# The last group's three output stores: from SyncE's queue to GpSimd's and ScalarE's, the last copy shared by two engines

## The chip, the cores and the metric

The kernel runs on one core of a Trainium2 chip. The metric is the device time of one execution in microseconds, over runs of the same program. Besides the runs there is one execution taken by the hardware profiler, with its own time and its own span.

A core has five engines that run side by side, each with its own instruction stream: TensorE (PE in the profile: matmuls, and PEld for their weight loads), VectorE (DVE), ScalarE (ACT), GpSimd (POOL) and SyncE (SP). They wait for each other through semaphores. A transfer between memory and the core's buffers (a DMA) is issued by an instruction on SyncE, ScalarE or GpSimd. The profile names an engine with a q behind it (SPq, POOLq, PEldq) where it means its instruction queue: issues of transfers, waits, branches and the like.

## The reference

An RWKV attention with a decaying state, and behind it a two-layer feed-forward network on its output:

```python
for t in range(S):                                   # batch 4, 8 heads, 768 steps, head size 48
    cur = np.einsum('bhd,bhe->bhde', u[None] * kt, vt)
    y[:, :, t] = np.einsum('bhd,bhde->bhe', rt, state + cur)
    state = wt[:, :, :, None] * state + np.einsum('bhd,bhe->bhde', kt, vt)

h = x @ w_in                                         # x: 3072 tokens x 384, w_in: 384 x 2048
g = h * (1.0 / (1.0 + np.exp(-1.702 * h)))
return (g @ w_out).astype(np.float32)                # w_out: 2048 x 384
```

Everything is float32. The output is 3072 x 384 floats; the kernel writes it transposed, as three blocks of 128 features by 3072 tokens (`out_t`).

## The kernel before

The 3072 tokens are 24 chunks of 128, and four chunks make a group of 512 tokens: six groups. The attention of a chunk leaves its output in the tile `x` of its group. The feed-forward of a group is cut into 16 tasks, one for each 128 of the 2048 hidden features: the first product (`first_product` or `first_rows`, into PSUM tile `ph`), the gelu on ScalarE and VectorE (`gelu`, L383 to L385), and the second product (`second_product`, L398 to L400, or `second_rows`, L424), which adds into three PSUM tiles of the group, `po0`, `po1` and `po2`, each 128 features by 512 tokens. The list `TASKS` has 106 tasks. The order of all pieces is written out: by the string `RAMP` at the start, then by the generator `rest()`, whose tokens (`l` load, `a` attention, `g`, `h`, `y`, `r` for the products and the gelu) are run one by one by `do`.

When the last task of a group has gone through the second product, `do` calls `store` (L493). It takes the three `po` tiles in turn: ScalarE copies and rescales one into an SBUF tile `ob` (L498, one of three buffers), and a transfer of 256 KB takes `ob` to the output (L499). For five groups the products run in halves of the array (`r` tokens) and the order of the tiles is 1, 0, 2; for the last group it is `y105` that ends it, with the order 0, 1, 2. Of this last group the matmuls of `po0`, `po1` and `po2` end one after the other, so the three copies follow them at the very end of the program.

Which queue issues a transfer is set by `queue[0]`. In the loop over `rest()` it is GpSimd's, except for tokens of the last task:

```python
queue[0] = G if int(token[1:]) < len(TASKS) - 1 else nc.sync     # L605
```

So the stores of groups 1 to 4 go through GpSimd (12 of them; those of group 0 fall in `RAMP`, which uses SyncE), and those of group 5 through SyncE.

Behind the loop stands a test that was computed long before (L613 to L622): each engine loads a count from memory (L622, TENSOR_LOAD) and compares (L623, COMPARE_BRANCH). For these inputs every engine jumps over the whole slow path, some hundred lines of code, to the end of the program. There each engine settles the semaphores that it owns: SyncE those of the transfers by SyncE and ScalarE (L623 EVENT_SEMAPHORE, eight of them), GpSimd those of its own transfers (four waits and an INC_SWDGE_SEM at L623). Then SyncE waits for all of them (L720) and a rendezvous of all five engines, led by GpSimd, ends the program: each engine runs a DRAIN and reports, GpSimd collects the reports and lets all go. SyncE's resets can't pass a transfer by SyncE or ScalarE that has not landed, and SyncE's waits at L720 can't pass GpSimd's INC_SWDGE_SEM.

The program is scheduled by hand: the instructions of an engine stand in the order in which the tokens emit them, and the framework adds the waits.

Of the kernel before, what the change touches and what calls it, by code (L numbers as in the profile page):

```python
# [13 lines left out]
AF = mybir.ActivationFunctionType  # L14
ALU = mybir.AluOpType
# [5 lines left out]
NTOK = B * S  # L21
# [20 lines left out]
W_SCALE = 2.0 ** 8  # L42
# [8 lines left out]
TASKS = [(0, 0, 2, f) for f in range(5)]  # L51
# [35 lines left out]
def rwkv_ffn_kernel(ctx: ExitStack, tc, wkr, vp, vrk, ub, w_in, w_out, masks, vt, uc, out):  # L87
    nc = tc.nc
    V, A, G, T = nc.vector, nc.scalar, nc.gpsimd, nc.tensor
# [24 lines left out]
        out=after, in_=after, pattern=[[1, C]], base=0, channel_multiplier=-1,  # L114
# [6 lines left out]
    queue = [nc.sync]  # L121
# [371 lines left out]
    def store(i, start, N, order=range(NM)):  # L493

        for m in order:
            o = po[i][m]
            ob = pools["late"].tile([P, WIDE], F32, tag="ob", name="ob", bufs=3)[:, 0:N]
            A.activation(ob, o[:, 0:N], AF.Copy, scale=1.0 / W_SCALE)  # L498
            queue[0].dma_start(out[m, :, bass.ds(start, N)], ob)  # L499
        po.pop(i)  # L500
        xs.pop(i)

# [4 lines left out]
    with tc.manual_schedule():  # L507
# [17 lines left out]
        def do(token):  # L525
            kind, i = token[0], int(token[1:] or 0)
            told[token] = told.get(token, 0) + 1
            if kind in "lamwr":
                piece(kind, i)
                if kind == "w" and all(told.get(f"w{n}") == 4 for n in range(2 * NL)):  # L530
                    early.close()
                    pools["late"] = fast.enter_context(tc.tile_pool(name="late", bufs=2))
            elif kind == "f":
                fetch(i)
            elif kind == "x":
                group, col = where[i]
                if i == 1:
                    fill_x(xs[group], 0, 2 * C)
                elif i == 3:
                    fill_x(xs[group], 2 * C, 4 * C)  # L540
                elif col == CHUNKS[group] - 1:
                    fill_x(xs[group], 0, (col + 1) * C)
            elif kind == "u":
                nc.sync.dma_start(u_sb, ub)
            elif kind == "M":
                A.dma_start(hm[0:D], masks[0:D])
                A.dma_start(hm[HB:R2], masks[D:R])
                for sf in states:
                    G.memset(sf, 0.0)
            elif kind == "k":  # L550
                for _ in range(i):
                    keep_clock()
            elif kind == "g":
                first_product(i, TASKS[i])
            elif kind == "h":
                gelu(i, TASKS[i])
            elif kind == "y":
                second_product(i, TASKS[i])
            if kind == "y" or kind == "r" and told[token] == 2:
                i -= LAG if kind == "r" else 0  # L560
                parts.pop(i, None)
                group = TASKS[i][0]
                if i == last[group]:
                    store(group, starts[group] * C, CHUNKS[group] * C, (1, 0, 2) if kind == "r" else range(NM))

        def rest():

            begins = []
            for t, (i, col) in enumerate(where):
                n = len([x for x in TASKS if x[0] == i - 1])  # L570
                begins.append(last.get(i - 1, -1) + 1 - BEFORE - round((CHUNKS[i] - 1 - col) * n / CHUNKS[i]))
            done, plan = dict(told), {}
            for t, begin in enumerate(begins):
                late = 0
                for kind, step, half in PARTS:
                    token = f"{kind}{t + 2 * (kind == 'l')}"
                    if done.get(token, 0):
                        done[token] -= 1
                    elif kind != "l" or t + 2 < NT:
                        at_ = 2 * (step + begin) + half  # L580
                        if at_ < 2 * FIRST:
                            at_ = 2 * FIRST + late
                            late += 1
                        plan.setdefault(at_, []).append(token)
            for j in range(FIRST, len(TASKS) + LAG):
                for post in range(2):
                    if post and j <= SPLIT[-1] + 1:
                        yield f"r{j}"
                        if j > SPLIT[0]:
                            yield f"h{j - 1}"  # L590
                    if post and j < len(TASKS) and j not in SPLIT:
                        yield f"g{j}"
                        yield f"h{j}"
                    yield from plan.get(2 * j + post, ())
                if j <= SPLIT[-1] + 1:
                    yield f"r{j}"
                elif f"y{j - LAG}" not in told:
                    yield f"y{j - LAG}"
# [3 lines left out]
        steady.append(True)  # L602
        tiled.append(True)
        for token in rest():
            queue[0] = G if int(token[1:]) < len(TASKS) - 1 else nc.sync  # L605
            do(token)
        queue[0] = nc.sync

# [13 lines left out]
    n = nc.values_load(cnt, min_val=0, max_val=full)  # L622
    with tc.If(n < full):  # L623
# [5 lines left out]
        with tc.tile_pool(name="gp", bufs=1) as gp, tc.tile_pool(name="ob", bufs=2) as ob, tc.For_i(0, B, 1) as b:  # L629
# [33 lines left out]
            for half in range(2):  # L663
                xs[half] = xg[half]
                for f in range(NF):
                    task = half, 0, 3, f
                    first_product(f, task)
                    gelu(f, task)
                    second_product(f, task)
                store(half, b * S + half * 384, 384)  # L670
# [54 lines left out]
```

## Time and profile before

| what | us |
|---|---|
| median of 3 runs | 537.95 (537.9 to 539.91) |
| the profiled execution's own time | 539.33 |
| its span, first to last instruction | 537.7 |
| PE busy | 522.9 (97%) |
| ACT / DVE / POOL busy | 285.5 / 294.5 / 58.7 |
| last matmul ends, about | 530.6 |
| last copy of `po` on ScalarE | 530.64 to 531.25 |
| last store issued on SyncE's queue | 531.9 |

A row of a group view has the line, the engine, the operation, and the tile written with what is read, then the count. In the view of one source line the columns are the least, median and longest duration in nanoseconds, then the start of the first and of the last of these instructions in microseconds from the span's start. In the timeline and the chain of waits the first two numbers are start and duration in microseconds. A semaphore instruction's start is the moment its waits were fulfilled, so time spent waiting shows as a gap in front of it and not as its duration.

### The profile page before, as it was taken

To read this page: it belongs to the slowest core of one execution; us is meant where nothing else is said; L and a number is where in the kernel's file an instruction comes from. 1 tells how busy PE (TensorE), PEld (TensorE's weight loads), DVE (VectorE), ACT (ScalarE), POOL (GpSimd) and SP (SyncE) were. 2 spreads that over 40 slices of the span, in tenths; PEclk is the share of its full clock that TensorE was granted. 3 is DMA by queue.
4 is the path that set the end of the run, shared out by engine and by line. 5 is a ranking of instruction groups with operands and counts; after the bars stand their busy time and mean duration, and the time that the engine had idled before them with its cause. 6 is when DMAs were issued, how large, how long until landed. Compare 5 with 4: busy or idle time off the path is not lost.

```text
span 537.7 us, 11653 instructions
## 1 busy us (share of the span) xinstructions
PE 522.9 (97%) x4750; PEld 442.9 (82%) x4750; DVE 294.5 (55%) x454; ACT 285.5 (53%) x629; POOL 58.7 (11%) x119
## 2 busy tenths in 40 slices
PE   6999899999999999999999999999999999999994
PEld 2667799988888888788999999988999887888873
DVE  3999788989765471664564554566466321211210
ACT  1889678987564364465355365454464432322222
POOL 5030110000100001030003030103020002100000
PEclk9999989999999999999999999999999999999998
DMA  8979949333632431163211354213250001100001
GB/s 202 236 189 204 320 110 183 74 89 103 180 88 67 96 95 29 47 173 79 53 45 37 91 155 98 53 46 69 58 155 1 1 1 30 59 3 2 1 1 64
DMA packets 15308, 48.26 MB, mean 90 GB/s; under 512 B 3024, under 2 KB 5264, under 8 KB 15248
## 3 DMA queue, kind: packets, MB, share of 16 engines
q0 software_dynamic: 6368, 23.73, 18.7%
q1 hardware_dynamic: 8624, 23.42, 16.8%
q8 instruction: 39, 0.64, 0.5%
q10 hardware_dynamic: 256, 0.30, 0.3%
q14 instruction: 21, 0.17, 0.1%
HBM read 40.36 MB, written 4.72 MB: 84 GB/s over the span
## 4 chain that ended last, share of the span: by engine, by line
PE 92%; DVE 4%; DMA 1%; ACT 1%; POOL 1%; issue 1%; DVEq 0%; SPq 0%; POOLq 0%
PE po L424 26%; PE ph L424 24%; PE ph L372 4%; PE ps_y L335 4%; PE po L398 4%; PE ps_s L322 4%; PE ph L373 4%; PE ph L374 4%; PE po L400 4%; PE po L399 4%; PE idle L413 4%; PE ps_y L342 3%; PE ps_u L307 1%; DMA x<-x 1%; PE ps_d L260 1%; PE ps_t L286 1%
## 5 line engine op out<-in xcount | busy, mean ns | idle before, releaser
L424 PE MATMUL ph<-x,pair 64*128 64x512 f32 x1134 | 194.0, 387 | 0.0
L385 DVE TENSOR_TENSOR gl<-gf,gh 128x512 fp32r<-128x512 f32 (+1 forms) x106 | 67.5, 639 | 193.7 <-ACT gf L384 193.7
L424 PE MATMUL po<-gh,pair 64*128 64x512 f32 x768 | 164.6, 396 | 0.2 <-SPq L429 0.2
L424 PEld LDWEIGHTS ph<-x,pair 64*128 64x128 f32 x1134 | 146.5, 184 | 14.7
L383 ACT ACTIVATE gh<-ph 128x512 fp32r<-128x512 f32 (+1 forms) x106 | 59.0, 556 | 179.1 <-PE ph L424 149.9
L424 PEld LDWEIGHTS po<-gh,pair 64*128 64x128 f32 x768 | 96.5, 185 | 11.8 <-issue 1.2
L424 PE MATMUL po<-gl,pair 64*128 64x512 f32 x384 | 103.0, 388 | 0.0
L297 ACT ACTIVATE am<-ident,s 128x128 f32<-128x128 f32 x192 | 58.9, 393 | 2.5 <-PE ps_y L335 2.5
L384 ACT ACTIVATE gf<-ph 128x512 f32<-128x512 f32 (+1 forms) x106 | 58.5, 552 | 0.0
L424 PEld LDWEIGHTS po<-gl,pair 64*128 64x128 f32 x384 | 50.2, 184 | 6.0
L372 PE MATMUL ph<-x,pair 128*128 128x512 f32 (+1 forms) x129 | 46.3, 359 | 2.4 <-DMA x<-x 2.4
L373 PE MATMUL ph<-x,pair 128*128 128x512 f32 (+1 forms) x129 | 44.6, 345 | 0.0
L374 PE MATMUL ph<-x,pair 128*128 128x512 f32 (+1 forms) x129 | 44.5, 345 | 0.0
L398 PE MATMUL po<-gh,pair 128*128 128x512 f32 (+1 forms) x126 | 44.0, 349 | 0.1
L400 PE MATMUL po<-gl,pair 128*128 128x512 f32 (+1 forms) x126 | 42.8, 340 | 0.0
L399 PE MATMUL po<-gh,pair 128*128 128x512 f32 (+1 forms) x126 | 42.7, 339 | 0.0
L325 DVE COPY_PREDICATED am<-after,ps_s 128x512 f32<-128x512 int32 x48 | 32.6, 732 | 3.8 <-PE ps_s L322 3.3
L360 POOL DMA_DIRECT2D x<-x x30 | 15.3, 516 | 163.4 <-DVE x L203 163.4
L232 DVE TENSOR_TENSOR_SCAN lp<-wkr_t,d1r 112x516 f32<-112x516 f32 x24 | 29.5, 1229 | 5.1 <-POOL d1r L106 4.4
L413 PE MATMUL idle<-d1r 112*128 112x512 bf16 x107 | 27.4, 403 | 4.4 <-POOL d1r L106 4.4
L372 PEld LDWEIGHTS ph<-x,pair 128*128 128x128 f32 x129 | 25.0, 194 | 6.7 <-issue 3.6
L238 DVE TENSOR_TENSOR_SCAN lp<-wkr_t,d1f 112x516 f32<-112x516 f32 x24 | 29.5, 1230 | 0.5
(75 smaller groups left out, 666.2 us busy)
## 6 DMA issues: line engine op xcount, KB each, us to landing
wkr_t<-in_wkr POOLq DMA_DIRECT2D x23, 288.9 KB, 6.2
raw<-in_w_out SPq DMA_DIRECT2D x6, 1024.0 KB, 17.4
wkr_t<-in_wkr SPq DMA_DIRECT2D x14, 385.2 KB, 5.2
wkr_t<-in_wkr POOLq DMA_DIRECT2D x9, 385.2 KB, 5.1
rk_t<-in_vrk POOLq DMA_DIRECT2D x9, 384.0 KB, 5.5
out_t<-ob POOLq DMA_DIRECT2D x12, 256.0 KB, 2.8
v_t<-in_vrk SPq DMA_DIRECT2D x15, 192.0 KB, 6.2
rk_t<-in_vrk SPq DMA_DIRECT2D x7, 384.0 KB, 4.2
```

Of the source, the lines that this page charges most:

```text
L297: A.activation(x_[:, p], ident, AF.Copy, scale=s[:, 2 * p + h : 2 * p + h + 1])
L372: T.matmul(ph, h_, xs[i][:, 0, c, cs], start=c == 0, stop=False)
L373: T.matmul(ph, h_, xs[i][:, 1, c, cs], start=False, stop=False)
L374: T.matmul(ph, l_, xs[i][:, 0, c, cs], start=False, stop=c == NM - 1)
L383: A.activation(gh, ph, AF.Gelu_apprx_sigmoid, scale=1.0 / W_SCALE)
L384: A.activation(gf, ph, AF.Gelu_apprx_sigmoid, scale=1.0 / W_SCALE)
L385: V.tensor_tensor(gl, gf, gh.bitcast(F32), op=ALU.subtract)
L398: T.matmul(o, h_, gh, start=first, stop=False, skip_group_check=True)
L399: T.matmul(o, l_, gh, start=False, stop=False, skip_group_check=True)
L400: T.matmul(o, h_, gl, start=False, stop=f == NF - 1, skip_group_check=True)
L413: T.matmul(out, zeros[:, 0:P], zeros[:, 0:WIDE], start=first, stop=first, skip_group_check=True)
L424: mm = T.matmul(out, w[rows], x[rows], start=start, stop=stop, skip_group_check=True)
```

## The change

All in the last group's stores. `queue[0]` stays GpSimd's for the last task too, so the copies of `po0` and `po1` are stored through GpSimd's queue. The last tile, `po2`, is copied in two halves of 256 columns: ScalarE does the left half, VectorE the right half, both into the same `ob` tile. Its store is issued from ScalarE's queue. SyncE issues no store of the last group. The slow path is not touched, since `start` isn't an integer there.

```diff
@@ store
         for m in order:
             o = po[i][m]
             ob = pools["late"].tile([P, WIDE], F32, tag="ob", name="ob", bufs=3)[:, 0:N]
-            A.activation(ob, o[:, 0:N], AF.Copy, scale=1.0 / W_SCALE)
-            queue[0].dma_start(out[m, :, bass.ds(start, N)], ob)
+            end = m == order[-1] and isinstance(start, int) and start + N == NTOK
+            n = N // 2 if end else N
+            A.activation(ob[:, 0:n], o[:, 0:n], AF.Copy, scale=1.0 / W_SCALE)
+            if end:
+                V.tensor_scalar(ob[:, n:], o[:, n:N], 1.0 / W_SCALE, None, op0=ALU.mult)
+            (A if end else queue[0]).dma_start(out[m, :, bass.ds(start, N)], ob)
         po.pop(i)
         xs.pop(i)
@@ the loop over rest()
         for token in rest():
-            queue[0] = G if int(token[1:]) < len(TASKS) - 1 else nc.sync
+            queue[0] = G
             do(token)
```

Lines behind the edit move by four: L622 of before is L626 of the change, L623 is L627, L720 is L724, and L498 and L499 are L500 and L503.

How the instructions stand on three engines at the program's end follows. DMASW and DMAHW in the waits are counts of landed transfers (GpSimd's, and those of SyncE and ScalarE).

GpSimd, from the stores of the fifth group (`ob` filled from `po` of group 4) to its branch. Before:

```order
L499 DMA out_t<-ob 128x512 [waits DMASW5_49,Activation_49]
L499 DMA out_t<-ob 128x512 [waits DMASW6_49,Activation_49]
L499 DMA out_t<-ob 128x512 [waits DMASW7_49,Activation_49]
L622 TENSOR_LOAD acc [waits DVE_49,Activation_49,Pool_49]
L623 COMPARE_AND_BRANCH
```

With the change:

```order
L503 DMA out_t<-ob 128x512 [waits DMASW5_49,Activation_49]
L503 DMA out_t<-ob 128x512 [waits DMASW6_49,Activation_49]
L503 DMA out_t<-ob 128x512 [waits DMASW7_49,Activation_49]
L503 DMA out_t<-ob 128x512 [waits DMASW0_49,Activation_49]
L503 DMA out_t<-ob 128x512 [waits DMASW1_49,Activation_49]
L626 TENSOR_LOAD acc [waits DVE_49,Activation_49,Pool_49]
L627 COMPARE_AND_BRANCH
```

Two stores of the last group now stand ahead of GpSimd's load, its branch and all that it does behind the branch.

ScalarE, from the last gelu to its branch, before and with the change:

```order
L384 ACTIVATE gf<-ph 128x512 [waits DVE_49]
L498 ACTIVATE ob<-po_5959 128x512 [waits DMASW5_49,PE_49]
L498 ACTIVATE ob<-po_5945 128x512 [waits DMASW6_49,PE_49]
L498 ACTIVATE ob<-po_5961 128x512 [waits DMASW7_49,PE_49]
L622 TENSOR_LOAD acc [waits DVE_49,Activation_49,Pool_49]
L623 COMPARE_AND_BRANCH
```

```order
L384 ACTIVATE gf<-ph 128x512 [waits DVE_49]
L500 ACTIVATE ob<-po_5959 128x512 [waits DMASW5_49,PE_49]
L500 ACTIVATE ob<-po_5945 128x512 [waits DMASW6_49,PE_49]
L500 ACTIVATE ob<-po_5961 128x256 [waits DMASW7_49,PE_49]
L503 DMA out_t<-ob 128x512 [waits DMAHW4_49,DVE_49]
L626 TENSOR_LOAD acc [waits DVE_49,Activation_49,Pool_49]
L627 COMPARE_AND_BRANCH
```

The third copy is half as wide, and a store that waits for VectorE stands between it and ScalarE's load and branch.

VectorE at the same place has one new row, and SyncE has lost three. VectorE with the change, then SyncE before and with it:

```order
L385 TENSOR_TENSOR gl<-gf,gh 128x512 [waits PE_49,Activation_49] x18
L502 TENSOR_SCALAR ob<-po_5961 128x256 [waits DMASW7_49,DMAHW2_49,DMASW2_49,Activation_49]
L626 TENSOR_LOAD acc [waits DVE_49,Activation_49,Pool_49]
L627 COMPARE_AND_BRANCH
```

```order
L622 ISA x2
L499 DMA out_t<-ob 128x512 [waits PE_49,DMAHW4_49,Activation_49]
L499 DMA out_t<-ob 128x512 [waits DMAHW5_49,Activation_49]
L499 DMA out_t<-ob 128x512 [waits DMAHW6_49,Activation_49]
L623 COMPARE_AND_BRANCH
```

```order
L626 ISA x2
L627 COMPARE_AND_BRANCH [waits PE_49]
```

VectorE's half waits for ScalarE and not for TensorE: the count of ScalarE's that it waits for is the one that the left half sets. SyncE's branch has no store ahead of it any more.

## The prediction

> **What bounds the kernel now.** I read the page first, then the chain of waits at the end, then the queues' views of the lines at the end.
>
> ```profile
> span 537.7 us, 11653 instructions
> PE 522.9 (97%) x4750; PEld 442.9 (82%) x4750; DVE 294.5 (55%) x454; ACT 285.5 (53%) x629; POOL 58.7 (11%) x119
> PE 92%; DVE 4%; DMA 1%; ACT 1%; POOL 1%; issue 1%; DVEq 0%; SPq 0%; POOLq 0%
> ```
>
> TensorE is busy for 97% of the span and carries 92% of the chain. The change touches none of its work, so nothing before the last copies can move. What is at stake is the tail. The chain's last pieces (start, duration, what), and SyncE's timeline over the whole tail and from 531 us on:
>
> ```profile
> 530.38 0.24 PE po L400
> 530.62 0.02 issue
> 530.64 0.60 ACT ob L498
> ...
> 529.91 2.33 SPq L499 DMA_DIRECT2D out_t<-ob  x3
> ...
> 530.59 1.66 SPq L499 DMA_DIRECT2D out_t<-ob  x2
> ```
>
> The last matmul ends at 530.62 and the last copy at 530.64 + 0.60 = 531.24. The span ends at 537.7, so 6.5 us of tail follow. The view of L499 in the last 10 us (least, median, longest ns, first and last start), and below it the same line around 468 us, where the fifth group was stored by GpSimd:
>
> ```profile
> L499 SPq DMA_DIRECT2D out_t<-ob x3: 342/383/1179, 529.9 to 531.9; - x3
> DMA to landing us min/median/max: 3.0/3.0/3.4
> ...
> L499 POOL DMA_DIRECT2D out_t<-ob x3: 542/564/573, 467.0 to 468.3; - x3
> DMA to landing us min/median/max: 2.3/2.6/3.0
> ```
>
> The second store's issue began at 530.59, the third's at 531.9 and lasted 383 ns: one issue took 1179 ns and held the third back by 0.65 us after its data was ready. The third landed by 531.9 + 3.0 = 534.9. Was that what SyncE waited for? The view of the branch line, queue by queue:
>
> ```profile
> L623 SPq EVENT_SEMAPHORE  x8: 17/17/17, 535.5 to 536.0; - x8
> L623 POOLq EVENT_SEMAPHORE  x4: 17/43/43, 469.5 to 471.3; - x4
> L623 POOLq COMPARE_BRANCH  x1: 58/58/58, 469.0 to 469.0; - x1
> L623 POOLq INC_SWDGE_SEM  x1: 2276/2276/2276, 471.4 to 471.4; - x1
> L623 DVEq COMPARE_BRANCH  x1: 72/72/72, 528.4 to 528.4; - x1
> L623 PEldq COMPARE_BRANCH  x1: 3822/3822/3822, 529.1 to 529.1; - x1
> L623 DVEq EVENT_SEMAPHORE  x1: 21/21/21, 531.5 to 531.5; - x1
> L623 ACTq COMPARE_BRANCH  x1: 45/45/45, 531.5 to 531.5; - x1
> L623 ACTq EVENT_SEMAPHORE  x1: 17/17/17, 532.0 to 532.0; - x1
> L623 SPq COMPARE_BRANCH  x1: 53/53/53, 532.3 to 532.3; - x1
> L623 PEldq EVENT_SEMAPHORE  x1: 51/51/51, 533.0 to 533.0; - x1
> ```
>
> No. SyncE branches at 532.3, behind its third store, and its next instruction runs at 535.5: a jump of 3.2 us, 0.6 longer than the landing. VectorE's and TensorE's jumps also take 3.1 (528.4 to 531.5) and 3.9 us (529.1 to 533.0); ScalarE's and GpSimd's take 0.5. So SyncE's late branch bounds the tail: 532.3, jump to 535.5, eight resets to 536.1, then twelve waits, and the rendezvous:
>
> ```profile
> L720 SPq EVENT_SEMAPHORE  x14: 17/28/28, 536.1 to 537.6; - x14
> L720 POOLq EVENT_SEMAPHORE  x4: 17/17/17, 536.9 to 537.6; - x4
> L720 POOLq DRAIN  x3: 50/107/8556, 473.7 to 537.4; - x3
> L720 SPq DRAIN  x3: 7/7/13, 536.8 to 537.1; - x3
> ```
>
> GpSimd collects the reports at 536.9, and the program ends 0.8 us later. The row to look at is the third: of GpSimd's three DRAINs one took 8.556 us. It is the one at 473.7, just behind INC_SWDGE_SEM (471.4 + 2.28 = 473.7), and it ended at 482.3, with 54 us to spare. GpSimd had issued its last transfer at 468.3.
>
> **The change part by part.** The sum is made against the profiled execution: span 537.7, own time 539.33, which is 1.4 above the median of 537.95. A shift of the span is added to the median.
>
> *SyncE loses three issues.* Its last work before them is the relay of TensorE's split tasks, at 524.3:
>
> ```profile
> L429 SPq EVENT_SEMAPHORE  x7: 17/17/28, 519.2 to 524.3; - x7
> ```
>
> It branches there, and its 3.2 us jump is over at 527.6, before the first of the last copies. This takes the present end of the chain off the path. What is late next, in turn:
>
> *Copy and store of po2.* These rows price them:
>
> ```profile
> L384 ACT ACTIVATE gf<-ph 128x256 f32<-128x256 f32 x20 | 7.6, 380 | 0.0
> L385 DVE TENSOR_TENSOR gl<-gf,gh 128x256 fp32r<-128x256 f32 x20 | 8.2, 416 | 5.8 <-ACT gf L384 5.8
> L613 DVE TENSOR_SCALAR acc<-acc 128x48 f32<-128x48 f32 x1 | 0.2, 180 | 0.0
> L127 ACTq DMA_DIRECT2D wkr_t<-in_wkr x2: 384/496/607, 0.9 to 2.3; - x2
> ```
>
> The left half is a 128x256 ACTIVATE: 0.38, to 531.02. The right half waits for it (the order above), so the halves run one behind the other. A 128x256 TENSOR_SCALAR from PSUM isn't in the trace: between 0.18 (48 columns) and 0.42 (256 columns, two inputs); I take 0.4, nearest in width, and the tile is whole at 531.45, against 531.24 before. The sharing costs 0.2 us instead of saving it. ScalarE then issues (0.4 to 0.6, or 1.2 as SyncE once did), 0.4 us earlier than SyncE's third at 531.9. By SyncE's 3.0 it lands at 534.5 (3.4: 534.9). SyncE's reset of that count (the fifth of eight, 535.8 before) can follow then, with the rest, 1.9 us to the end. If this set the end, the span would be 536.4, a gain of 1.3.
>
> ScalarE's and VectorE's loads and branches move behind this work:
>
> ```profile
> L622 POOLq TENSOR_LOAD <-acc x1: 644/644/644, 468.3 to 468.3; - x1
> L622 DVEq TENSOR_LOAD <-acc x1: 540/540/540, 527.8 to 527.8; - x1
> L622 ACTq TENSOR_LOAD <-acc x1: 731/731/731, 530.7 to 530.7; - x1
> ```
>
> VectorE: 531.45 + 0.6 + a jump of 3.1 = 535.2. ScalarE: 531.45, issue 0.5, load 0.8, jump 0.5 = 533.2; if its jump became as long as TensorE's 3.9, 536.6. All are due at the rendezvous, 536.9 before, so they cost nothing while that is not earlier.
>
> *GpSimd gets two stores, and behind them its whole ending.* This is the term that decides. The second store waits for the second copy, whose end released SyncE's second issue at 530.59, so GpSimd issues it at 530.6. What followed GpSimd's last store before is all in rows: issue 468.3, landing at most 3.0 later, INC_SWDGE_SEM 471.4, 2.28 us of it, DRAIN at 473.7 for 8.56, free at 482.3. From issue to free: 14.0 us. Its load (0.64) and its branch (0.5) lie under the landing. Set behind 530.6: landing 533.6, INC_SWDGE_SEM 533.7 to 536.0, DRAIN 536.0 to 544.55. GpSimd must be through its DRAIN to collect the reports, so the rendezvous moves from 536.9 to 544.55 and the span ends 0.8 later, at 545.35. That is **+7.65 us**. Before, TensorE's 54 us covered all of it; now nothing does. SyncE's twelve waits need GpSimd's INC_SWDGE_SEM: they run from 536.0 to 536.8, under the DRAIN.
>
> Sum: all that SyncE's free branch and the earlier last store give (at most 1.3) is hidden under GpSimd, and 537.95 + 7.65 = **545.6 us**, 1.4% slower.
>
> The DRAIN can't be split by the trace: it may pay for the transfers just settled, or run only as long as something else lets it. From below, the rows with nothing to settle are 50 and 107 ns. From above, 8.56 plus what may grow: a GpSimd jump like TensorE's 3.9 would put its waits at 530.6 + 0.7 + 3.9 = 535.2 instead of under the landing at 533.6, so +1.6. I take 8.56: the same instruction behind the same INC_SWDGE_SEM, and a 2.28 us INC that sets the same eight counts.
>
> One rule of the notes speaks the other way. The Trainium skill (VectorE: DVE Perf Modes, "The DRAIN you can't avoid") knows a boilerplate DRAIN on all five engines that is a constant 12 ns or so. SyncE's 7 to 13 ns agree with it, GpSimd's 8556 ns does not, and the measurement decides. By the rule the time would be that of the second rival.
>
> **The rivals.**
>
> *The DRAIN comes back shorter.* Half-way between 0.1 and 8.56, at 4.3 us, GpSimd is free at 540.3: +3.4, or 541.4. For: its length has no cause in the trace, and at 473.7 the other engines worked beside it while at 536 they are idle. Against: I see no row that ties it to their work. Chance 0.08.
>
> *The DRAIN does not come back: not slower.* One mechanism: the 8.56 us belongs to something that was only due at 473.7, and the DRAIN behind the last stores is as short as the others (0.05 to 0.11 us). Then SyncE, which waits for INC_SWDGE_SEM's end at 536.0 instead of starting its twelve waits at 536.1, sets the end: −0.1, or 537.85. If INC_SWDGE_SEM were short too, the ScalarE store's landing would set it: −1.3, 536.6. It decides below a DRAIN of 0.9 us (536.0 to 536.9). For: two of three DRAINs are short, and INC_SWDGE_SEM took 27 ns when it ran with no transfers yet:
>
> ```profile
> L713 POOLq INC_SWDGE_SEM  x1: 27/27/27, 0.2 to 0.2; - x1
> L713 POOLq DRAIN  x1: 186/186/186, 0.5 to 0.5; - x1
> ```
>
> Against: the short ones, this one too, stand where no transfer of GpSimd's had been made since the last settling. Chance 0.15, with the rule above in it.
>
> *Faster beyond the noise.* 537.95 less 0.5% is 535.25. It needs 2.7 us, and the best sum above, with GpSimd free, gives 1.3. Chance 0.02.
>
> **How the numbers follow.** Forecast 0.75 at 545.6; the shorter DRAIN 0.08 at 541.4; no DRAIN 0.15 at 536.6 to 537.9; faster 0.02. The forecast's own range: 0.7 below (a landing at 2.3 instead of 3.0) is 544.9; 1.6 above (a long GpSimd jump, or a landing that late) is 547.2, and the runs before spread by 2 (537.9 to 539.91), so 547.6. To hold 8 in 10 it goes down to the shorter DRAIN: **541.4 to 547.6**. About 0.5%, 2.7 us, is what a measurement of this kernel can tell from no change. Slower by more than that: the forecast and the shorter DRAIN, 0.83. Within it: 0.15. Faster: 0.02.
>
> **What would show it.** In the changed kernel's profile: POOLq DRAIN at L724 with one of some 8.5 us, starting near 536.0; POOLq INC_SWDGE_SEM of about 2.3 us starting 3 us after GpSimd's last issue; POOLq EVENT_SEMAPHORE at L724 first at about 544.6 and the span near 545.4; SPq EVENT_SEMAPHORE at L724 from 536.0, so SyncE is ready 8 us ahead of the end. SyncE's COMPARE_BRANCH should stand at 524 or so, VectorE's TENSOR_SCALAR at 531.0 behind the 0.38 ACTIVATE and not beside it, and ScalarE's store near 531.5. I am wrong if the long DRAIN is gone or much shorter, or if it starts right behind the branch instead of behind the landings; the halves side by side, or a long issue on ScalarE, would be wrong steps that leave the time as it is.

## The result, and the profile after

The change makes the kernel slower. In runs side by side the kernel before has a median of 540.35 us (6 runs, 537.9 to 541.95) and the changed one of 547.59 us (6 runs, 545.66 to 550.25). The ratio is 1.0144, with a 95% interval of 1.0101 to 1.0187. By the interval the change costs 5.5 to 10.1 us. The forecast was 545.6 us against 537.95, a ratio of 1.0142.

The page of the changed kernel, for comparison with the span and the chain shown of before:

```profile
span 547.4 us, 11656 instructions
PE 522.6 (95%) x4750; PEld 443.0 (81%) x4750; DVE 294.9 (54%) x455; ACT 285.3 (52%) x629; POOL 59.8 (11%) x121
```

TensorE's busy time is what it was (522.6 against 522.9), but the span is 9.7 us longer. Two pairs of rows tell where these arose. First the copies of the last group, in the views of their source lines, of before and then of the change:

```profile
L498 ACT ACTIVATE ob<-po x3: 597/598/598, 529.3 to 530.6; 128x512 f32<-128x512 f32 x3
```

```profile
L500 ACT ACTIVATE ob<-po x3: 384/598/598, 530.8 to 532.1; 128x512 f32<-128x512 f32 x2, 128x256 f32<-128x256 f32 x1
...
L502 DVE TENSOR_SCALAR ob<-po x1: 424/424/424, 532.5 to 532.5; 128x256 f32<-128x256 f32 x1
...
L503 POOL DMA_DIRECT2D out_t<-ob x2: 542/542/542, 531.7 to 532.3; - x2
L503 ACTq DMA_DIRECT2D out_t<-ob x1: 382/382/382, 533.0 to 533.0; - x1
DMA to landing us min/median/max: 2.8/3.1/3.3
```

The first of the three copies starts at 529.3 before and at 530.8 after: 1.5 us of the 9.7 arose ahead of anything that the change touches. They arose at 62 to 70 us, in one wait of TensorE's. The view of TensorE's waits between 55 and 75 us, of before and of the change:

```profile
PE ph L372 <- DMA x<-x: 2.4, 1, 2.4
```

```profile
PE ph L372 <- DMA x<-x: 4.2, 1, 4.2
```

The wait is 1.8 us longer, of which 1.5 are left by 75 us and stay. So the two profiled executions differ by 1.5 us before the tail. I therefore measure the tail by itself from here on: from the start of the first of the last three copies to the span's end. It is 537.7 − 529.3 = 8.4 us before and 547.4 − 530.8 = 16.6 us after. **The tail grew by 8.2 us.**

The branch line and the end of the program in the changed kernel (L627 and L724; least, median, longest ns, first and last start):

```profile
L627 SPq EVENT_SEMAPHORE  x8: 17/17/17, 528.3 to 536.5; - x8
...
L627 SPq COMPARE_BRANCH  x1: 53/53/53, 525.8 to 525.8; - x1
...
L627 DVEq COMPARE_BRANCH  x1: 72/72/72, 533.9 to 533.9; - x1
...
L627 POOLq INC_SWDGE_SEM  x1: 2302/2302/2302, 535.5 to 535.5; - x1
L627 DVEq EVENT_SEMAPHORE  x1: 21/21/21, 539.2 to 539.2; - x1
...
L724 SPq EVENT_SEMAPHORE  x14: 17/28/957, 537.7 to 547.3; - x14
L724 POOLq EVENT_SEMAPHORE  x4: 17/17/17, 546.6 to 547.3; - x4
L724 POOLq DRAIN  x3: 46/107/8719, 537.8 to 547.1; - x3
```

GpSimd's ending now stands at the end of the program: its last issue at 532.3, INC_SWDGE_SEM at 535.5 for 2.30 us, the long DRAIN at 537.8 for 8.72 us, the reports collected at 546.6, the end at 547.4. SyncE branched at 525.8 and was back from its jump at 528.3. The last thing that it waited for ahead of the rendezvous was not GpSimd's INC_SWDGE_SEM but VectorE: one of its waits took 957 ns and ended when VectorE had come back from its jump at 539.2. SyncE, the last engine but GpSimd, reached its first DRAIN at 539.4, so all others were ready 7 us ahead of GpSimd.

### The profile page after: what moved, and what is told of

The parts are those of the page before. It is cut to its first block, busy times and chain, and to the rows that moved or that the text cites. A ratio compares the mean times of both kernels' runs of the same rounds, so it can differ in the third digit from the quotient of the medians.

```text
span 547.4 us, 11656 instructions
## 1 busy us (share of the span) xinstructions
PE 522.6 (95%) x4750; PEld 443.0 (81%) x4750; DVE 294.9 (54%) x455; ACT 285.3 (52%) x629; POOL 59.8 (11%) x121
## 4 chain that ended last, share of the span: by engine, by line
PE 90%; DVE 4%; DMA 1%; ACT 1%; POOL 1%; issue 1%; DVEq 0%; SPq 0%; POOLq 0%
PE po L424 25%; PE ph L424 23%; PE ph L372 4%; PE ps_y L335 4%; PE po L398 4%; PE ps_s L322 4%; PE ph L373 4%; PE ph L374 4%; PE po L400 4%; PE po L399 4%; PE idle L413 3%; PE ps_y L342 3%; PE ps_u L307 1%; DMA x<-x 1%; PE ps_d L260 1%; PE ps_t L286 1%
## 5 line engine op out<-in xcount | busy, mean ns | idle before, releaser
L360 POOL DMA_DIRECT2D x<-x x30 | 15.3, 516 | 163.4 <-DVE x L203 163.4
```

## The experiments

The two theories at first. A: GpSimd's ending (landing, INC_SWDGE_SEM, DRAIN) is the price of any store that GpSimd issues at the end. B: the price lies in the shared copy or in the store on ScalarE's queue. What is read in each run is the tail, because the part ahead of it differs between executions: the first of the last copies starts at 527.3 to 532.3 us in the profiles of ten kernels whose fast path is the same up to there. A ratio is to the kernel before, run beside it (medians of 539.98 us for e1, e2, e3 and e7, and 540.56 for e8 and e11). The others are single profiled executions without a ratio, and only the tail and the durations in the profile are used. The expectations of e1, e2, e3 and e7 count the tail from the end of the last matmul; that is 1.3 us less than the tail here (7.1 against 8.4 before, 15.3 against 16.6 with the change). The code is shown against the kernel before, in e8 and e9 against the change, and ... stands for lines that are left out.

**e1: the shared copy, and no store on GpSimd.** The first two stores go through SyncE, the third through ScalarE, the third copy is shared as in the change.

```diff
+            end = isinstance(start, int) and start + N == NTOK
+            n = N // 2 if end and m == 2 else N
-            A.activation(ob, o[:, 0:N], AF.Copy, scale=1.0 / W_SCALE)
-            queue[0].dma_start(out[m, :, bass.ds(start, N)], ob)
+            A.activation(ob[:, 0:n], o[:, 0:n], AF.Copy, scale=1.0 / W_SCALE)
+            if end and m == 2:
+                V.tensor_scalar(ob[:, n:], o[:, n:N], 1.0 / W_SCALE, None, op0=ALU.mult)
+            ((nc.sync, nc.sync, A)[m] if end else queue[0]).dma_start(out[m, :, bass.ds(start, N)], ob)
```

> The change with its two GpSimd stores given back to SyncE; the split copy of po2 and ScalarE's store stay. The tail is counted from the end of the last matmul to the span's end: 7.1 us before (530.6 to 537.7), 15.3 with the change (532.1 to 547.4). Theory A (GpSimd's ending sets the end: landing, INC_SWDGE_SEM of 2.3, DRAIN of 8.6): GpSimd's long DRAIN is back near 475 and the tail is 6.0 to 8.2 us, set by VectorE's branch, which the split puts 1.8 us behind the last matmul, and its jump of 3.1 (before) to 5.3 us (with the change). Theory B (the split and ScalarE's store, with the late jumps behind them, cost the time): the tail stays at 14 us or more.

Measured: 541.13 us against 539.98, ratio 1.0023 (0.9996 to 1.0051). The tail is 9.6 us. In the views of the branch line and the end:

```profile
L627 POOLq INC_SWDGE_SEM  x1: 2276/2276/2276, 473.0 to 473.0; - x1
...
L627 DVEq COMPARE_BRANCH  x1: 72/72/72, 533.8 to 533.8; - x1
...
L627 DVEq EVENT_SEMAPHORE  x1: 21/21/21, 539.5 to 539.5; - x1
L724 SPq EVENT_SEMAPHORE  x14: 17/28/772, 538.2 to 540.5; - x14
```

With GpSimd's ending back at 473 us, where TensorE's work covers it, 7.0 of the 8.2 us are gone. B falls as the cause of these. But the tail is 1.2 us longer than before, and most of it is in the rows: VectorE's branch at 533.8 is followed by its next instruction at 539.5. This is a jump of 5.7 us, not 3.1, and SyncE waited 0.77 us for it. The other 0.4 is SyncE's own jump, 4.1 us here (533.5 to 537.6) against 3.2 before, less what its earlier branch gained.

**e2: the same without the shared copy.** Stores on SyncE, SyncE and ScalarE, ScalarE copies the whole of `po2`.

```diff
+            end = isinstance(start, int) and start + N == NTOK
...
-            queue[0].dma_start(out[m, :, bass.ds(start, N)], ob)
+            ((nc.sync, nc.sync, A)[m] if end else queue[0]).dma_start(out[m, :, bass.ds(start, N)], ob)
```

The first of these lines stands in e3, e5, e7 and e10 to e13 too.

> SyncE stores po0 and po1, ScalarE copies all of po2 and stores it; no split, VectorE has nothing. Theory A: SyncE branches behind its second issue, some 1.2 us behind the last matmul, jumps for 3.2 and needs 2.2 for the rest: a tail of 6.6 us, 0.5 shorter than before, which the times can't tell. VectorE branches early again, so no wait for it. Theory B without the split: also 6.6; with ScalarE's store as the cost: over 8.

Measured: 540.37 us, ratio 1.0011 (0.9985 to 1.0037), tail 8.4 us, as before, and 0.5 more than expected.

```profile
L624 SPq EVENT_SEMAPHORE  x8: 17/17/17, 538.3 to 538.8; - x8
...
L624 DVEq COMPARE_BRANCH  x1: 72/72/72, 531.3 to 531.3; - x1
...
L624 DVEq EVENT_SEMAPHORE  x1: 21/21/21, 534.1 to 534.1; - x1
L624 SPq COMPARE_BRANCH  x1: 53/53/53, 534.3 to 534.3; - x1
```

VectorE, free ahead of the copies, jumps in 2.8 us. SyncE, with a store less, branches 2.2 us behind the start of the first copy (532.1 to 534.3), against 3.0 before. But its jump now takes 4.0 us (534.3 to 538.3) against 3.2, which uses up the 0.8.

**e3: one store on GpSimd, nothing else.** `po0` through GpSimd, the other two through SyncE, no shared copy.

```diff
...
+            ((G, nc.sync, nc.sync)[m] if end else queue[0]).dma_start(out[m, :, bass.ds(start, N)], ob)
```

> The kernel before with one edit: po0's store of the last group goes through GpSimd, po1's and po2's through SyncE as before. Theory A: one store is enough. It is issued 0.4 us before the last matmul ends, GpSimd is free 14.0 to 14.2 us behind the issue and the program ends 0.8 later: a tail of 14.5 us, 7.4 longer than before, and a DRAIN of 8.6 to 8.7. If the DRAIN grows with the stores just settled, it is some 4 us and the tail 10. Theory B: nothing of the split is here, so 7.1.

Measured: 547.64 us, ratio 1.0148 (1.0104 to 1.0192), tail 15.8 us.

```profile
L624 POOLq INC_SWDGE_SEM  x1: 2296/2296/2296, 535.1 to 535.1; - x1
...
L721 POOLq EVENT_SEMAPHORE  x4: 17/17/17, 546.1 to 546.8; - x4
L721 POOLq DRAIN  x3: 50/107/8637, 537.4 to 546.6; - x3
```

One small edit, one store of 256 KB, and 7.4 of the 8.2 us are there; the rest is mostly that the change issues its second store 0.7 us later behind the first copy than e3 its only one. Theory A holds: what costs is not the number of stores at the end, but that there is one. The DRAIN's length, though, has a pattern: 8556 ns before, 8637 here with one GpSimd transfer more, 8719 in the change with two more. That is 81 and 82 ns for each.

**e7: no store on GpSimd, and one on SyncE only.** `po0` through SyncE, the other two through ScalarE, no shared copy.

```diff
...
+            ((nc.sync, A, A)[m] if end else queue[0]).dma_start(out[m, :, bass.ds(start, N)], ob)
```

> SyncE stores po0 alone, ScalarE copies all three and stores po1 and po2; GpSimd and VectorE have nothing of the last group. Theory A: GpSimd's ending is hidden again, SyncE's jump begins about 0.3 us before the last matmul ends and is over 3 us later, before the last landing. ScalarE issues po1's store between its copies, so the last copy ends 1.0 us and the last store is issued 1.1 us behind the last matmul, lands 3.0 later, and 1.9 us follow: a tail of 6.0, 1.1 shorter than before and too little for the times to show (0.2%). If ScalarE's jump becomes long (3.6 to 5.3 as on TensorE and VectorE), the tail is 7 to 8. Theory B: the store on ScalarE costs, tail over 8.

Measured: 539.0 us, ratio 0.9988 (0.9964 to 1.0013). The tail is 6.8 us in the one profile, the shortest of all with every store in it, 1.6 us below before and 0.5 below what was expected.

```profile
L624 SPq EVENT_SEMAPHORE  x8: 17/17/17, 535.9 to 536.9; - x8
...
L500 ACTq DMA_DIRECT2D out_t<-ob x2: 368/375/382, 533.2 to 534.3; - x2
L500 SPq DMA_DIRECT2D out_t<-ob x1: 341/341/341, 532.5 to 532.5; - x1
DMA to landing us min/median/max: 2.6/3.0/3.0
```

SyncE's eight resets, which took 0.5 us in one go before, now stretch from 535.9 to 536.9: they wait for the last landing, 534.3 + 2.6 = 536.9. No issue is long any more (341 to 382 ns, against 1179 for the second when SyncE issued all three). By the whole time it can't be told from before, since the interval holds 1.

**e6: the shared copy with the last group's stores left out.** It leaves out the three stores, so 512 of the 3072 tokens are not written; the copies are made.

```diff
...
+            if not end:
+                queue[0].dma_start(out[m, :, bass.ds(start, N)], ob)
```

> The split copy stays, but the three stores of the last group are left out (so 512 tokens of the output aren't written): VectorE branches as late as with the change, while nothing moves to memory. VectorE's jump took 3.1 us where it began ahead of the stores and 5.3 and 5.7 us where it ran beside them. If the stores' traffic stretches it: 3.1 to 3.6 here. If it is the late start itself, beside TensorE's and ScalarE's jumps: 5 or more. No GpSimd store here, so its DRAIN is near 475 and the span from the first copy's start is 6.5 to 7.5 us by the first and 8.5 to 9 by the second.

Measured: a tail of 7.6 us (529.4 to 537.0).

```profile
L628 DVEq COMPARE_BRANCH  x1: 72/72/72, 532.3 to 532.3; - x1
...
L628 DVEq EVENT_SEMAPHORE  x1: 21/21/21, 535.9 to 535.9; - x1
L725 SPq EVENT_SEMAPHORE  x14: 17/28/3836, 527.8 to 536.9; - x14
```

VectorE's jump takes 3.6 us when no store is under way, against 5.2 to 5.7 in four kernels with the same shared copy and the stores. It still sets the end: SyncE waited 3.8 us for it. So of the 2.6 us by which the jump grew from before to e1, about 2.1 go with the stores, and 0.5 come from elsewhere.

**What does GpSimd's DRAIN pay for?** The first idea was INC_SWDGE_SEM: it would count up the same semaphores that GpSimd would have raised in the slow path, and the DRAIN might complete that.

**e8: the change, with no transfer of GpSimd's in the slow path**, so that the two ways through the program have the same count and no INC_SWDGE_SEM is made. The list `slow` is filled where the slow path begins in the program's text; the slow path is not run for these inputs.

```diff
+    slow = []
...
-        (other or G).dma_start(dst[HB:R2], src[D:R])
+        (other or (nc.sync if slow else G)).dma_start(dst[HB:R2], src[D:R])
...
+    slow.append(True)
```

> The change, with the GpSimd transfers of the slow path alone (which is never run here) moved to SyncE. The one GpSimd transfer of the run before left no INC_SWDGE_SEM and a DRAIN of 3.0 us, so the 11 us may not belong to the stores. Theory A2: INC_SWDGE_SEM only makes GpSimd's counts what they would be behind the slow path (416 more over eight counts), and the DRAIN is its execution; without such transfers in the slow path both go, GpSimd is free some 4 us behind its last issue, and the time from the first copy's start to the span's end falls from 16.6 to 9.6 us, where VectorE's late jump sets it (9.6 with the stores on SyncE and the split). Theory A1: the DRAIN settles the 106 transfers that GpSimd made; 16.6 stays.

Measured: 543.81 us against 540.56, ratio 1.0065 (1.0036 to 1.0093), tail 12.6 us.

```profile
L629 POOLq COMPARE_BRANCH  x1: 58/58/58, 532.9 to 532.9; - x1
...
L726 POOLq EVENT_SEMAPHORE  x4: 17/17/17, 542.3 to 543.0; - x4
L726 POOLq DRAIN  x3: 50/107/8803, 533.4 to 542.8; - x3
```

INC_SWDGE_SEM is gone and the DRAIN is as long as ever (8803 ns). It starts right behind the branch, 0.5 us after it, and no longer behind the landing and the 2.3 us: 4.0 us less tail. The expectation had 9.6 us by the idea and 16.6 against it; 12.6 is neither. So INC_SWDGE_SEM is a second price and not the cause of the first, and that idea falls.

**e9: the change, with 12 of the slow path's 26 transfers left to GpSimd**, those of the weights (192 of the 416 counts that INC_SWDGE_SEM makes up for by the idea, 16 for each transfer). The others go through SyncE.

```diff
...
-        (other or G).dma_start(dst[HB:R2], src[D:R])
+        (other or (nc.sync if slow else G)).dma_start(dst[HB:R2], src[D:R])
...
-                (queue[0], G)[i].dma_start(
+                (queue[0], nc.sync if slow else G)[i].dma_start(
...
```

> The same, but the slow path keeps its 12 GpSimd loads of weights: the counts differ by 192 instead of 416, still over eight of them. A2 with a price by the amount added: INC_SWDGE_SEM and DRAIN together 5.1 us instead of 11.0, and 10.7 us from the first copy's start to the end. A2 with a price by the count: 11.0 and 16.6. A1: 11.0 and 16.6.

Measured: a tail of 16.0 us; the 0.6 less than in the change lie between GpSimd's last issue and INC_SWDGE_SEM (2.5 us, against 3.1).

```profile
L629 POOLq INC_SWDGE_SEM  x1: 2316/2316/2316, 531.4 to 531.4; - x1
...
L726 POOLq DRAIN  x3: 50/107/8719, 533.8 to 543.1; - x3
```

Less than half of the counts are left, and neither duration moves. They don't go with the counts added.

**e4: no transfer on GpSimd at all**: every load, move and store of its queue goes through SyncE.

```diff
-        (other or G).dma_start(dst[HB:R2], src[D:R])
+        (other or nc.sync).dma_start(dst[HB:R2], src[D:R])
...
-            queue[0] = G if int(token[1:]) < len(TASKS) - 1 else nc.sync
+            queue[0] = nc.sync
```

> The kernel before with every GpSimd transfer of the whole program moved to SyncE (loads, weights, the moves inside x, stores), so GpSimd makes none; SyncE's queue gets crowded and the span longer, which is not compared. Read is GpSimd's ending alone. If the long DRAIN belongs to the settling of its own transfers: no INC_SWDGE_SEM at the end and all DRAINs under 0.2 us. If it belongs to GpSimd's jump to the program's end, or to the program's end as such: a DRAIN of about 8.6 us stays.

**e5: e4, and `po0`'s last store on GpSimd**, the only transfer of GpSimd's in the program.

```diff
...
+            ((G, nc.sync, nc.sync)[m] if end else queue[0]).dma_start(out[m, :, bass.ds(start, N)], ob)
```

> The same, but po0's store of the last group through GpSimd: its only transfer, against 116 in the kernel before and 118 with the change. If the ending is a fixed price of having used GpSimd's queue: INC_SWDGE_SEM of 2.3 and DRAIN of 8.6 us, and from the first copy's start to the span's end 15.8 us (8.4 before, 15.8 with one GpSimd store beside all the others). If the price grows with the transfers made since the start: a DRAIN well under 1 us and 8.4 us.

**e10: e5 with the slow path as before**, so that INC_SWDGE_SEM is there.

```diff
...
-                (queue[0], G)[i].dma_start(
+                (queue[0], G if slow else nc.sync)[i].dma_start(
...
```

> As the run with one GpSimd transfer in all (po0's store of the last group), but the slow path keeps its GpSimd transfers. A2: INC_SWDGE_SEM is back (416 added) and with it 2.3 + 8.6 us, 15.8 from the first copy's start. A1: one transfer to settle, so a DRAIN of 3 us or less. Loads go through SyncE, so the span isn't compared.

Measured: the whole times are 562.61, 565.91 and 563.31 us, with all of GpSimd's transfers now on SyncE's queue; they tell nothing of the tail. The DRAIN in the three, e4, e5, e10:

```profile
L720 POOLq DRAIN  x3: 34/41/82, 468.7 to 560.6; - x3
```

```profile
L624 POOLq COMPARE_BRANCH  x1: 45/45/45, 557.6 to 557.6; - x1
...
L721 POOLq DRAIN  x3: 34/93/3023, 557.8 to 563.9; - x3
```

```profile
L626 POOLq INC_SWDGE_SEM  x1: 178/178/178, 556.3 to 556.3; - x1
...
L723 POOLq DRAIN  x3: 34/93/139, 556.5 to 561.5; - x3
```

Without a transfer the longest DRAIN has 82 ns, and with a single one that has landed it has 139 ns, where the same store behind 104 others (e3) has 8637 ns. In e5 it starts 0.2 us behind the branch, while its store is still on the way, and takes 3.0 us. It ends at 560.8, 3.8 us behind the store's issue, and the landings of the last three stores took 3.6 to 3.7: without INC_SWDGE_SEM the DRAIN itself seems to wait for the transfer. In e10 the slow path has all of its 26 transfers, and the DRAIN stays at 139 ns, so transfers that are in the program and not run don't count. The length belongs to something that collects over the program. The expectation of e5 speaks of 116 to 118 transfers; counted in the view of groups there are 104 before and 106 in the change:

```profile
L360 POOL DMA_DIRECT2D x<-x x30 | 15.3, 516 | 163.4 <-DVE x L203 163.4
L127 POOL DMA_DIRECT2D wkr_t<-in_wkr x23 | 12.2, 529 | 120.4 <-DVE kq L254 95.6 <-DVE acc L613 18.7 <-DMA raw<-in_w_in 5.7
L499 POOL DMA_DIRECT2D out_t<-ob x12 | 6.6, 552 | 67.3 <-ACT ob L498 67.0 <-issue 0.2
L170 POOL DMA_DIRECT2D raw<-in_w_in x12 | 6.5, 547 | 0.0
L153 POOL DMA_DIRECT2D v_t<-in_vrk x9 | 5.2, 581 | 38.9 <-PE ps_y L335 38.9
L156 POOL DMA_DIRECT2D rk_t<-in_vrk x9 | 5.0, 555 | 0.1
L126 POOL DMA_DIRECT2D wkr_t<-in_wkr x9 | 4.8, 535 | 19.2 <-DVE kq L254 19.2
```

30 + 23 + 12 + 12 + 9 + 9 + 9 = 104.

**e11: two stores on GpSimd, one on ScalarE, no shared copy, no transfer of GpSimd's in the slow path.** It is e8 without the shared copy.

```diff
...
+            ((G, G, A)[m] if end else queue[0]).dma_start(out[m, :, bass.ds(start, N)], ob)
```

> The change's queues (GpSimd, GpSimd, ScalarE) without the split copy and without GpSimd transfers in the slow path: SyncE and VectorE branch early, ScalarE copies all of po2 and issues its store 2.0 us behind the first copy's start, landing 3.0 to 3.2 later, then 1.9 to the end: 6.9 to 7.1 us, against 8.4 before and 6.8 with one store on SyncE and two on ScalarE. 1.4 us are 0.26%, under what the times tell; A1 would give 16.

Measured: 544.09 us, ratio 1.008 (1.0049 to 1.0112), tail 12.6 us, as in e8. The expectation of about 7 us missed: it took the DRAIN to go with INC_SWDGE_SEM. The DRAIN again has 8803 ns, from 535.2. It sets the end whether the copy is shared or not.

**e12 and e13: few transfers, and small ones or large ones.** In e12 GpSimd keeps only the 42 moves `x<-x` (12 of them went through SyncE before) and `po0`'s last store: 43 transfers. In e13 it keeps everything but the 30 moves, and has `po0`'s last store: 75 transfers. The slow path is as before in both, so INC_SWDGE_SEM stands there and the DRAIN runs behind the landing.

The line of the moves in e12, then in e13:

```diff
...
-                (queue[0], G)[i].dma_start(
+                (queue[0] if slow else G, G)[i].dma_start(
...
```

```diff
...
-                (queue[0], G)[i].dma_start(
+                (nc.sync, G if slow else nc.sync)[i].dma_start(
...
```

> GpSimd keeps the 42 x<-x moves and issues po0's last store (43 transfers by GpSimd since the start); all its other fast-path transfers go through SyncE; the slow path is as before, so INC_SWDGE_SEM stands behind the landing. The whole time is not compared, since SyncE is loaded with the rest; what is read is the length of INC_SWDGE_SEM and of the DRAIN behind it. Theory by number of transfers (57 ns and 81.7 ns for each, through the runs with 1, 104, 105 and 106): DRAIN 3.57 us, INC_SWDGE_SEM about 1.0 us. Theory by packets (8556 ns for 6368 packets before; a move has 48, a store 80, here 2096): DRAIN about 2.85 us. Theory of a step (either on or off): 8.6 us or 0.14 us.

> The other side of the run before it: the x<-x moves go through SyncE, all other transfers of GpSimd's stay with it, with two of the last group's stores as in the change; 75 transfers by the count of the order (75 by number, some 5000 packets). By number of transfers: DRAIN 6.18 us, INC_SWDGE_SEM about 1.7 us. By packets: DRAIN about 6.7 us. Step: 8.6 or 0.14 us. If the two runs lie on the line through 1 and 104 transfers, the price belongs to the number of transfers that GpSimd made since the start, whatever they carry.

Two slips in these expectations: e13 has one of the last group's stores on GpSimd and not two (the 75 are right), and the packets were counted wrongly. The queue's rows have 6368 packets before, 1424 in e12 and 5488 in e13, so a price by packets would be 1.9 and 7.4 us; by the megabytes in the same rows it would be 0.9 and 8.0. The rows of before, e12 and e13 (packets, MB, share):

```profile
q0 software_dynamic: 6368, 23.73, 18.7%
```

```profile
q0 software_dynamic: 1424, 2.62, 2.5%
```

```profile
q0 software_dynamic: 5488, 22.22, 16.0%
```

Measured, e12 and then e13 (whole times 550.54 and 569.07 us, which again tell of SyncE's queue):

```profile
L626 POOLq INC_SWDGE_SEM  x1: 1037/1037/1037, 543.1 to 543.1; - x1
...
L723 POOLq DRAIN  x3: 40/107/3579, 544.2 to 548.3; - x3
```

```profile
L626 POOLq INC_SWDGE_SEM  x1: 1691/1691/1691, 558.7 to 558.7; - x1
...
L723 POOLq DRAIN  x3: 46/107/6187, 560.5 to 567.2; - x3
```

3579 and 6187 ns, where the price by number gave 3.57 and 6.18 us; not a step, not the packets and not the bytes. All kernels with an INC_SWDGE_SEM on one line:

| transfers by GpSimd | kernel | INC_SWDGE_SEM, ns | DRAIN, ns |
|---|---|---|---|
| 1 | e10 | 178 | 139 |
| 43 | e12 | 1037 | 3579 |
| 75 | e13 | 1691 | 6187 |
| 104 | before, e1, e2, e6, e7 | 2276 | 8556 |
| 105 | e3 | 2296 | 8637 |
| 106 | change, e9 | 2302, 2316 | 8719 |

From 1 to 104 the DRAIN grows by (8556 − 139) / 103 = 81.7 ns for each transfer, and INC_SWDGE_SEM by (2276 − 178) / 103 = 20.4 ns. Each transfer that GpSimd made since the start, whatever it carried and however long it had landed, costs 0.10 us at the end of its stream in these kernels. What GpSimd does in that time no run shows.

The tails beside each other:

| kernel | stores of po0, po1, po2 | third copy | first copy starts, span ends, us | tail, us |
|---|---|---|---|---|
| before | SP, SP, SP | whole | 529.3, 537.7 | 8.4 |
| change | GpSimd, GpSimd, ScalarE | shared | 530.8, 547.4 | 16.6 |
| e3 | GpSimd, SP, SP | whole | 531.2, 546.9 | 15.8 |
| e9 | as the change | shared | 527.3, 543.3 | 16.0 |
| e8 (no INC_SWDGE_SEM) | as the change | shared | 530.5, 543.1 | 12.6 |
| e11 (no INC_SWDGE_SEM) | GpSimd, GpSimd, ScalarE | whole | 532.3, 544.9 | 12.6 |
| e1 | SP, SP, ScalarE | shared | 531.0, 540.6 | 9.6 |
| e2 | SP, SP, ScalarE | whole | 532.1, 540.5 | 8.4 |
| e7 | SP, ScalarE, ScalarE | whole | 531.9, 538.6 | 6.8 |

The tails are taken from unrounded times, so a difference of the two columns can be off by 0.1.

## Why the prediction was right, and where it was wrong

*GpSimd's ending comes back at full length, behind the last stores: right.* 14.0 us from issue to free were taken from the rows at 468 us; it was 546.5 − 532.3 = 14.2. The parts: landing and reset 3.1 (taken 3.1), INC_SWDGE_SEM 2.30 (2.28), DRAIN 8.72 (8.56), the rendezvous 0.8 (0.8). What the prediction left unexplained is now measured: the 8.56 us paid for 104 transfers, and the change brought two more.

*The issue at 530.6: mis-sized by 0.3.* The prediction took the start from SyncE's row, which issued about 0.03 us after the copy had ended. In the change the second copy ends at 532.04, but GpSimd issues at 532.33, 0.29 us later; its first store stands as far behind the first copy. This, 0.16 of the DRAIN and 0.1 of all smaller parts together make 7.65 into the 8.2 that the tail grew.

*The time: 2.0 us too low, by the base.* The step that failed is the sum's first term, 537.95 as the time without the change. In the runs beside the changed kernel the same kernel had 540.35, so this term was 2.4 us too small. The other term, the growth of 7.65, is 7.24 between the medians (5.5 to 10.1 by the interval) and 8.2 by the tails of the two profiles. By the medians, 2.4 too little and 0.4 too much make the 2.0. That the ratio came out within 0.0002 of the forecast is in part luck, with an interval of 0.0086. The runs shown spread by 2 us and I let that into the upper end of the range only, while the forecast stood on their low end. The upper end took this spread and the 1.6 us of a late landing or long jump as alternatives; three of the six changed runs (548.95, 548.97 and 550.25) lie above its 547.6. In the two profiles the 1.5 us come from the wait for `x<-x` at 62 us. That this one wait makes the spread of all the runs is not shown: e2 has 2.2 us of it, and its copies still start at 532.1. What the ten traces do show is that the spread arises early: the shift of ScalarE's instructions against before, from −2.0 us in e9 to 3.0 in e11 at the first of the last copies, is already there at 105 us and changes by no more than 0.1 after that. What causes it stays open.

*The rivals.* The DRAIN that comes back shorter would have needed fewer transfers, as in e12. The rival that it does not come back fell with the change itself and with e3: the rows with 50 and 107 ns stand where nothing had been issued since the DRAIN before them. The rule that the prediction weighed (the Trainium skill, VectorE: DVE Perf Modes, "The DRAIN you can't avoid", a boilerplate DRAIN that is constant at about 12 ns) fits the other four engines here, 7 to 17 ns, and does not fit GpSimd, whose DRAIN went from 139 to 8719 ns with the transfers made. That section of the Trainium skill speaks of DRAINs from the runtime's preamble and postamble; those here carry a line of the program (L720), so it may not be about them.

*The prices of those rivals: wrong.* Without GpSimd's ending the prediction had the change 0.1 to 1.3 us faster. Here e1 shows the shared copy and ScalarE's store without it, with two stores on SyncE: a tail 1.2 us longer. In the change itself VectorE was back only at 539.2, 8.4 us behind the first copy, where the whole tail of before had ended. The step that failed is "VectorE: 531.45 + 0.6 + a jump of 3.1 = 535.2". The jump took 5.3 us in the change and 5.7 in e1, and the load ahead of it 0.8 in the change. I had set aside a long jump for ScalarE, whose jump stayed short (534.4 to 534.8 in the change), and none for VectorE. The forecast was not hurt, since GpSimd's DRAIN ran until 546.5 and hid it.

*The shared copy: right.* The halves ran one behind the other (0.38 from 532.1, then 0.42 from 532.5), and the tile was whole 0.2 us later than one copy of 0.6 would have made it. The TENSOR_SCALAR, bounded between 0.18 and 0.42, took 0.424: the upper end, where 0.4 was taken.

*SyncE: right, and worth nothing here.* Branch at 525.8, back at 528.3, a jump of 2.5 us that is fully hidden. ScalarE's issue took 382 ns and not the 1.2 us that was the bad case.

## What to carry to other kernels

In this program a store near the end did not cost what its transfer takes, but what its engine still had to do behind it. Before a last store goes to GpSimd's queue, count the transfers that GpSimd has made in the whole program: here about 0.08 us of DRAIN for each followed behind the last one, and where the program settles semaphores of an untaken path 0.02 us more, which is hidden only as long as the other engines still work. One of the last stores on SyncE and two on ScalarE (e7) shortened the tail by 1.6 us in one profile, which the run times can't confirm; two on SyncE and one on ScalarE (e2) did not shorten it. And sharing a small copy with an otherwise free engine made that engine's jump late and longer.

## What the runs showed of the hardware that was not expected

GpSimd's DRAIN at the end of the program remembers. 42 moves whose last was issued at 462 us made the DRAIN at 544 us (e12) 3.4 us longer than that behind a single store (e10). It grows by 81.7 ns for each transfer of GpSimd's since the start, from 1 to 106 of them, in all kernels with an INC_SWDGE_SEM.

A jump to the end of the program is not one price. ScalarE's and GpSimd's stay at 0.5 us or less. VectorE's took 2.8 to 3.1 us when it came ahead of the last copies (before, e2), 3.6 behind them without stores (e6), and 5.3 and 5.7 beside the stores (the change, e1); SyncE's took 2.5 ahead of the stores (the change), 3.2 behind its own three (before), 4.0 in e2 and 4.1 in e1. The Trainium skill (Runtime: NRT & Kernel Launch, "Instruction fetch mechanics") says that a taken branch to a target outside the pages already fetched has to wait for a fetch by DMA; the microseconds on the long jumps here agree with that. The traces also have the packets of a queue of the kind `instruction` (q14 on the page), 8 KB each, and VectorE's jumps hold one or more of them. The last one there starts 1.0 us behind the branch and takes 0.5 before, 1.2 and 0.8 in e6, 1.9 and 1.7 in the change, 2.4 and 1.6 in e1; VectorE's next instruction follows 1.5 to 1.7 us behind its end. So this packet's start and length make most of the difference between the jumps. That it is VectorE's is read from the times alone, since packets are not named by engine. In the change the last packet of the stores ended at 535.4 and this one ran from 535.8 to 537.5: its late start fits a wait behind the stores, its length does not, and that stays open, as does why the jumps of ScalarE and GpSimd are short.
